# A 128-row K tile loaded by transfers of 64, 32, 16 and 8 rows, once in each of two layers

## The chip, the core and the metric

The kernel runs on one core of a Trainium2 chip. The core has engines that run beside each other, each with its own instruction stream: TensorE (PE, with its weight loads PEld), VectorE (DVE), ScalarE (ACT), GpSimd (POOL) and SyncE (SP), which issues the data transfers. Sixteen DMA engines carry them. The on-chip memory has 128 rows (partitions). The metric is the time of one execution on the device in microseconds (us); lower is better.

## The reference

Two layers, each an attention block over a cache and a small mixer block, for one new token in each of two batch entries:

```python
def _A_ref(x, k_cache, v_cache, wq, wo):
    B, Sq, D = x.shape            # 2, 1, 576
    H, Dh = 32, 128
    q = (x @ wq).reshape(B, Sq, H, Dh).transpose(0, 2, 1, 3)
    scores = jnp.einsum("bhqd,bhkd->bhqk", q, k_cache) * (Dh ** -0.5)
    p = _softmax(scores, axis=-1)
    o = jnp.einsum("bhqk,bhkd->bhqd", p, v_cache)
    return o.transpose(0, 2, 1, 3).reshape(B, Sq, H * Dh) @ wo
...
x = A_x
x = x + _A_ref(_layernorm(x, axis=-1), A_k_cache, A_v_cache, A_wq, A_wo)
x = x + _B_ref(_layernorm(x, axis=-1), B_w1, B_w2, B_w3, B_w4)
x = x + _A_ref(_layernorm(x, axis=-1), A_k_cache, A_v_cache, A_wq, A_wo)
x = x + _B_ref(_layernorm(x, axis=-1), B_w1, B_w2, B_w3, B_w4)
return x
```

The caches are [2, 32, 16384, 128] in bf16. Each of the 2 x 32 = 64 units (one head of one batch entry) has a K of 4 MB and a V of 4 MB, and both layers read all of them: 2 x 64 x 8 MB, apart from five tiles that the second layer still finds on the chip whole or in part. `_B_ref` adds small products with w1 to w4 (576 and 4608 wide).

## The kernel before

**Tiles.** The K or the V of a unit is one tile: 128 rows of 32 KB, where row p holds 128 neighbouring positions of 128 values. `mem` has six slots for such tiles (`NSLOT`, L334, L376). `plan_all` writes down all transfers of the kernel in the order in which they are to be issued, each with its place in `mem`: `plan_tile` (L426) and `plan_piece` (L435) for the caches, others for the weights. A tile in one piece is one entry with one transfer of 128 rows and the semaphore of its slot (`tile0` to `tile5`). The order is K of a unit, then V of the unit before (`tile_order`, L569). Layer 0 takes the units from 0 to 63, layer 1 takes 62, 63, 61 and then 0 to 60 (`order`, L565).

**Issue.** `Store.pump` (L286) hands out the entries in order, as soon as the slot of the first one is free; `Store.release` (L322) frees a slot when the last instruction that reads it is placed, and pumps again. `Graph.dma` (L88) makes of an entry one SyncE operation that starts each transfer of its list, and each adds 16 to the semaphore when it has landed (L101); the value that readers wait for is counted by the number of transfers:

```python
self.dma_count[sem] += 16 * len(starts)
o.val = self.dma_count[sem]
h = self.dma_sems[sem]

def fn(sp):
    for dst, src in starts:
        sp.dma_start(dst, src).then_inc(h, 16)
```

All transfers stand on SyncE's one queue, in the order of the plan.

**Landing.** `landed` (L1194) places a relay on GpSimd: it waits for the tile's semaphore and tells TensorE, and for K tiles VectorE too. In the profile a wait for the relay is named POOLq L202.

**Attention of one unit.** Half of a K tile's columns are transposed on TensorE (L1241), copied out by ScalarE (L1253) and multiplied with the query (L1267); VectorE does the other half with an elementwise product (L1287) and a sum (L1291). Then come the maximum over all rows on GpSimd (L1307), the exponentials on ScalarE (L1319, L1322), and the product with V on TensorE (L1361). Most units run inside loops on the three compute engines; SyncE and GpSimd are written out in full. A unit's V is used one unit later than its K.

**Between the layers and at the end** the weights wo, w3, w4, wq (and w1 at the end) pass through the same slots in smaller pieces, and the products with them (L874, L751, L768) follow each other.

The first small weight, w2, is loaded at the start by two transfers: four blocks of 128 rows of 1152 B, and a tail of 64 rows of 1152 B, which go to rows 64 to 127.

Of the kernel before, what the change touches and what calls it, by code (L numbers as in the profile page):

```python
# [328 lines left out]
class KB:  # L329
# [11 lines left out]
    PARKED = 5  # L341
    GONE = 72
    RAW = 2
    TURNS = {("w3", 0): 1, ("w3", 1): 1, ("w3", 2): 1, ("w4", 1): 1, ("w4", 3): 1, ("w4", 6): 1, ("w4", 8): 1,
             ("wq", 0): 1, ("wq", 1): 1, ("wq", 2): 1}

# [25 lines left out]
    def _alloc(self):  # L372
# [44 lines left out]
        self.quad = misc[:, 20:24]  # L417
        self.raw = misc[:, 24:24 + self.RAW * (1 + 3 * B) // 2].bitcast(BF16).rearrange("p (k c) -> p k c", k=self.RAW)
        self.cor = [self.prod[:, 1280 + 2 * MT * B * i:1280 + 2 * MT * B * (i + 1)].bitcast(FP32) for i in range(2)]
# [3 lines left out]
        self.mps = ps("mps", [128, 512], FP32)  # L423


    def plan_tile(self, t, u, slot, cuts=(), skip=0):  # L426

        b, hh = u % self.B, u // self.B
        src = (self.K if t == "k" else self.V)[b, hh].rearrange("(p j) d -> p (j d)", p=128)
        cuts = [0, *cuts, self.NB]  # L430
        for a, z in zip(cuts[:-1], cuts[1:]):
            if a >= skip:
                self.plan_piece(t, u, slot * self.TILE, src, a, z - a)

    def plan_piece(self, t, u, base, src, a, n):  # L435
        sem = f"tile{base // self.TILE}" if n == self.NB else f"piece{base // self.TILE}_{a}_{n}"
        self.store.plan((t, u, a, n), sem, base + 256 * a, 256 * n,
                        [(lambda m: m, src[:, a * 128:(a + n) * 128])])

    def plan_cols(self, nm, l, w, parts):  # L440

# [57 lines left out]
    def plan_all(self):  # L499

        T, U, n = self.TILE, self.U, self.KT - 1
        row, w3r, wqr = 2 * self.D, 2 * self.F, 2 * 128 * self.H
        H, MT = self.H, self.MT
        self.parts = {}
        self.plan_cols("wq", 0, self.wq, self.whole(self.wq, [4 * T + wqr * k for k in range(self.KT)]))
        self.plan_small("w2", 0, self.w2, 4 * T + wqr * n + wqr // 2, (0, 64))

        tiles = self.tile_order(0)
        place = [i % 6 for i in range(len(tiles))]
        place[-1] = 2  # L510
        half, quarter = self.BP, self.BP // 2
        for (t, u), slot in zip(tiles, place):
            self.plan_tile(t, u, slot, (half, half + quarter) if (t, u) == ("v", U - 1) else ())
        last = {tile: slot for tile, slot in zip(tiles, place)}
        third = U - self.CARRY - 1
        assert last["k", third] == 1 and last["v", third] == 4

        self.cuts = {}
        P = 4 * row
        a, c = [4 * T + P * i for i in range(4)], [T, T + P]  # L520
        assert 256 * self.GONE == 4 * P and 256 * 8 * self.PARKED >= 2 * P and 256 * 8 * self.NKT >= P
        turn = iter([*a, c[0]] + [a[0], a[1], c[1], a[2], a[3], c[0]] * 6)
        h = MT // 2
        self.cuts["wo", 0] = [(i, i + 4, next(turn)) for i in range(0, 32, 4)]
        halves = lambda n: [(k, m, z, next(turn)) for k in range(self.KT - 1) for m, z in ((0, n), (n, 2 * n))] + \
                           [(self.KT - 1, 0, 2 * n, next(turn))]
        w3 = halves(h)
        self.groups = [(0, 4, 8, 12, 16, 18), (0, 8, 12, 16, 18)]
        g = self.groups[0]
        self.cuts["w4", 0] = [(h * i + p, h * i + q, next(turn)) for i in range(2) for p, q in zip(g[:-1], g[1:])]  # L530
        self.plan_rows("wo", 0, self.wo, self.cuts["wo", 0])
        self.plan_cols("w3", 0, self.w3, w3)
        self.plan_groups("w4", 0, self.w4, self.cuts["w4", 0])
        self.plan_cols("wq", 1, self.wq, halves(H // 2))

        b, hh = third % self.B, third // self.B
        tiles = self.tile_order(1)
        b2, h2 = tiles[0][1] % self.B, tiles[0][1] // self.B
        for i in (1, 2, 3, None, 0):
            if i is None:  # L540
                self.plan_piece(*tiles[0], T, self.K[b2, h2].rearrange("(p j) d -> p (j d)", p=128), 0, quarter)
            else:
                self.plan_piece("v", third, 4 * T, self.V[b, hh].rearrange("(p j) d -> p (j d)", p=128),
                                i * self.GONE // 4, self.GONE // 4)
        place = [(3, 4, 5, 0, 2, 1)[i % 6] for i in range(len(tiles))]
        for i, (t, u) in enumerate(tiles):
            if (t, u) != ("v", third):
                self.plan_tile(t, u, place[i], (quarter, half, half + quarter) if i == 0 else
                               (half,) if i == len(tiles) - 1 else (), 0 if i else quarter)
        self.cuts["wo", 1] = [(0, 11, 2 * T), (11, 22, 2 * T + 11 * row), (22, 32, 0)]  # L550
        at = 10 * row
        w4_at = T + 2 * w3r + w3r // 2
        self.cuts["w4", 1] = [(0, 8, w4_at)] + \
                             [(a, b, 3 * T + (a - 8) * row) for a, b in ((8, 16), (16, 26), (26, 30), (30, 34), (34, 36))]
        self.plan_rows("wo", 1, self.wo, self.cuts["wo", 1])
        self.plan_cols("w3", 1, self.w3, self.whole(self.w3, [at, at + w3r, T, T + w3r, T + 2 * w3r]))
        self.plan_groups("w4", 1, self.w4, self.cuts["w4", 1])
        w1_at = 2 * T
        for i, k in enumerate((0, 2)):
            self.store.plan(("w1", 1, i), f"w1_{i}", w1_at + k * row, 2 * row, [  # L560
                (lambda m: m.rearrange("p (k n) -> p k n", n=self.D),
                 self.w1[k * 128:(k + 2) * 128, :].rearrange("(k p) n -> p k n", p=128))])
        self.store.plan(("w1", 1, 2), "w1_2", w1_at + 4 * row, row, [(lambda m: m[self.TL:, :], self.w1[4 * 128:, :])])
# [168 lines left out]
    def unscaled(self):  # L732

        R, B = self.RAW, self.B
        hi, lo = self.raw[:, :, 1:1 + B], self.raw[:, :, 1 + B:1 + 2 * B]
# [4 lines left out]
    def cols_chunk(self, w, l, k, out, pk, n, rhs, rk, cols, first, last=False, held=False):  # L740
# [15 lines left out]
        if l == (1 if w == "wq" else 0):  # L756
            self.turn(self.TURNS.get((w, k), 0), settle=not held)

# [60 lines left out]
    def hs_projection(self):  # L819
# [16 lines left out]
        self.copy_psum(self.hs, "hs")  # L836
        B, R = self.B, self.RAW
        self.dv(lambda e: e.tensor_copy(out=self.raw[:, :, 1 + 2 * B:], in_=self.hs[:, 0:R, :]),
# [22 lines left out]
    def rows_projection(self, w, l, rhs, rk):  # L861
# [4 lines left out]
        for i, (a, b, _) in enumerate(cuts):  # L866
# [14 lines left out]
            if l == 0:  # L881
                if (w, i) == ("wo", 1):
                    self.park(self.order(0)[self.U - self.CARRY - 1], self.NKT, self.PARKED)
                self.turn(self.TURNS.get((w, i), 0))

    def z_projection(self, l):
        B, KT, MT, R = self.B, self.KT, self.MT, self.RAW
        MB, w = MT * B, 1 + 3 * B
# [568 lines left out]
```

## Time and profile before

| | |
|---|---|
| time, median of 3 runs | 2550.05 us (2549.99 to 2550.48) |
| profiled execution, its time | 2549.84 us |
| profiled execution, its span | 2548.1 us, first to last instruction |
| DVE busy | 1897.0 us, 74% |
| PE / PEld busy | 1614.7 us, 63% / 1580.7 us, 62% |
| ACT busy | 1204.2 us, 47% |
| read from HBM | 1092.37 MB, 429 GB/s over the span |
| K tiles in one transfer | 124, median 40.7 us from issue to landing |
| V tiles in one transfer | 123, median 49.6 us from issue to landing |

How to read it: the span is cut into 40 equal slices of 63.7 us, and each digit is a busy share in tenths. "DMA" is the mean busy share of the 16 DMA engines, "GB/s" what they moved. "xN" counts instructions, packets or issues. "A <- B" reads "A waited for B". In the view of stretches ("755.84:1183.33 ...") the columns are the stretch, its length, the busy time and count of PE, PEld, DVE, ACT and POOL, the granted TensorE clock, the DMA share and GB/s. In the DMA view a packet is one row of a transfer, "under 512 B" are the marks at the end of each engine's part, and each queue's line has packets, MB and the share of 16 engines over the stretch. In the view of waits the numbers are us in total, times, and the longest in us.

### The profile page before, as it was taken

The page shows a single profiled execution, that of the slowest core. Times are in us where ns is not written, and L with a number is a line of the kernel's source. Part 1 is how long each engine was busy: PE and PEld are TensorE (multiplying, and loading weights), DVE is VectorE, ACT ScalarE, POOL GpSimd, SP SyncE. Part 2 cuts the span into 40 slices and gives each one's busy share as a digit, 9 for nine tenths or more (in the row PEclk, how much of TensorE's full clock was granted, in tenths as well). Part 3 has the DMA queues.
Part 4 walks back from the last instruction along what each step waited for, and adds up shares of the span by engine and source line. Part 5 has one row for each costly group of instructions (what it writes and reads, how often), then busy time and mean ns, then how long its engine had stood idle before and what let it go on. Part 6 is the DMA issues. An engine that isn't in the chain of part 4 may idle for free.

```text
span 2548.1 us, 74893 instructions
## 1 busy us (share of the span) xinstructions
PE 1614.7 (63%) x34407; PEld 1580.7 (62%) x34407; DVE 1897.0 (74%) x2062; ACT 1204.2 (47%) x1810; POOL 53.5 (2%) x151
## 2 busy tenths in 40 slices
PE   4666666656666666666777766656665666666566
PEld 3666666656666665666667666656665665666566
DVE  5877777777777777777648877777777777777774
ACT  3544544444454444445435544444454444445442
POOL 0000000000000000000000000000000000000000
PEclk8555555555555555555656555565555555555555
DMA  9999999999999999999999999999999999999999
GB/s 410 428 433 431 432 432 431 433 431 433 430 432 432 432 432 431 433 431 432 419 411 427 432 431 432 432 432 432 432 432 432 432 432 432 432 433 431 433 431 386
DMA packets 46928, 1093.19 MB, mean 429 GB/s; under 512 B 5140, under 2 KB 6296, under 8 KB 12440
## 3 DMA queue, kind: packets, MB, share of 16 engines
q1 hardware_dynamic: 46872, 1092.40, 100.0%
q8 instruction: 41, 0.67, 0.1%
q14 instruction: 15, 0.12, 0.0%
HBM read 1092.37 MB, written 0.00 MB: 429 GB/s over the span
## 4 chain that ended last, share of the span: by engine, by line
DMA 66%; DVE 23%; PE 5%; issue 5%; SPq 1%; ACT 0%; DVEq 0%; POOLq 0%
DMA mem<-in_A_k_cache_dram 63%; DVE s_dve L1291 12%; DVE prod L1287 9%; PE tps L1241 2%; PE mps L1361 2%; DMA mem<-in_B_w_dram 1%; DMA mem<-in_A_wo_dram 1%; PE sps L1267 1%; SPq L101 1%; PE sps L1212 1%; DVE diag L1208 0%; DVE l L1339 0%; DVE q_col L1205 0%; DMA mem<-in_A_wq_dram 0%; DVE mx L1302 0%
## 5 line engine op out<-in xcount | busy, mean ns | idle before, releaser
L1253 ACT ACTIVATE kt<-tps 128x1024 bf16<-128x1024 bf16 x992 | 1002.9, 1023 | 878.0 <-PE tps L1241 859.5
L1291 DVE TENSOR_REDUCE s_dve<-prod 128x16 f32<-128x2048 bf16 x504 | 1152.1, 2286 | 17.3
L1241 PE MATMUL tps<-ident,mem 128*128 128x128 bf16 x8192 | 1000.0, 300 | 141.3 <-POOLq L202 135.2
L1287 DVE TENSOR_TENSOR prod<-mem,qb 128x2048 bf16<-128x2048 bf16 x504 | 616.8, 1224 | 525.4 <-POOLq L202 493.9
L1361 PE MATMUL mps<-p,mem 128*128 128x1 bf16 x16384 | 512.2, 166 | 549.7 <-POOLq L202 519.3
L1241 PEld LDWEIGHTS tps<-ident,mem 128*128 128x128 bf16 x8192 | 761.3, 136 | 151.1 <-POOLq L202 145.0
L1361 PEld LDWEIGHTS mps<-p,mem 128*128 128x128 bf16 x16384 | 487.5, 104 | 558.3 <-ACT p L1322 552.2
L1267 PEld LDWEIGHTS sps<-q_col,kt 128*128 128x128 bf16 x7936 | 399.5, 113 | 0.8 <-ACT kt L1253 0.4
L1267 PE MATMUL sps<-q_col,kt 128*128 128x1 bf16 x7936 | 388.1, 170 | 0.4 <-issue 0.3
L1212 PE MATMUL sps<-diag,ones_bf 128*128 128x128 bf16 x127 | 36.5, 287 | 195.4 <-DVE diag L1208 195.4
L1212 PEld LDWEIGHTS sps<-diag,ones_bf 128*128 128x128 bf16 x127 | 13.2, 104 | 205.6 <-DVE diag L1208 205.6
L1316 ACT ACTIVATE mx<-mx 128x1 f32<-128x1 f32 x128 | 26.0, 203 | 236.2 <-POOL mx L1307 236.2
L1307 POOL PARTITION_ALL_REDUCE mx<-mx x128 | 51.1, 400 | 2441.9 <-DVE mx L1305 2323.7
L1215 ACT ACTIVATE qb<-sps 128x128 bf16<-128x128 f32 x127 | 35.2, 277 | 137.3 <-PE sps L1212 137.3
L1319 ACT ACTIVATE p<-s_dve,mx 128x64 bf16<-128x64 f32 x126 | 43.8, 348 | 4.1
L1253 ACT ACTIVATE mem<-tps 128x1024 bf16<-128x1024 bf16 x32 | 32.0, 1025 | 22.0 <-PE tps L1241 19.6
L1322 ACT ACTIVATE p<-sps,mx 128x64 bf16<-128x64 f32 x128 | 37.7, 294 | 0.1
L1302 DVE TENSOR_REDUCE mx<-sps 128x1 f32<-128x64 f32 x128 | 27.6, 216 | 7.5 <-PE sps L1267 7.5
L874 PE MATMUL mps<-prod,mem 128*128 128x2 bf16 x680 | 22.1, 166 | 14.5 <-DMA mem<-in_B_w_dram 8.8
L1208 DVE TENSOR_SCALAR diag<-ident,q_f 128x128 bf16<-128x128 bf16 x127 | 31.1, 245 | 0.0
L874 PEld LDWEIGHTS mps<-prod,mem 128*128 128x128 bf16 x680 | 20.6, 105 | 16.2 <-DMA mem<-in_B_w_dram 7.5
L707 ACT ACTIVATE misc<-misc 128x2 f32<-128x2 f32 x8 | 2.4, 296 | 51.4 <-DVE misc L705 51.4
(117 smaller groups left out, 293.4 us busy)
## 6 DMA issues: line engine op xcount, KB each, us to landing
mem<-in_A_k_cache_dram SPq DMA_DIRECT2D x124, 4096.0 KB, 40.7
mem<-in_A_v_cache_dram SPq DMA_DIRECT2D x123, 4096.0 KB, 49.6
mem<-in_B_w_dram SPq DMA_DIRECT2D x21, 576.0 KB, 7.7
mem<-in_B_w_dram SPq DMA_DIRECT2D x7, 1152.0 KB, 33.9
mem<-in_A_v_cache_dram SPq DMA_DIRECT2D x3, 2048.0 KB, 40.4
mem<-in_A_wq_dram SPq DMA_DIRECT2D x10, 512.0 KB, 6.5
mem<-in_A_wo_dram SPq DMA_DIRECT2D x8, 576.0 KB, 19.3
mem<-in_A_wq_dram SPq DMA_DIRECT2D x4, 1024.0 KB, 8.0
```

The lines of the kernel that those rows point to most:

```text
L874: ins = pe.matmul(self.mps[:, t * B:(t + 1) * B], lhsT=buf[:, o:o + 128], rhs=rhs(k), start=(k == 0 and t == 0), stop=(k == last), skip_gr ...
L1212: self.pe(lambda pe: pe.matmul(qps, lhsT=self.ones_bf[:, :], rhs=self.diag[:, :], start=True, stop=True, skip_group_check=True), reads=["o ...
L1215: self.act(lambda e: e.activation(out=self.qb[i][:, :], in_=qps, func=ACT.Copy), reads=[("qps", i)], writes=[("qb", i)], sig=("qb", i))
L1241: ins = pe.transpose(self.tps[t][:, j * 128:(j + 1) * 128], buf[:, j * 128:(j + 1) * 128], self.ident[:, :])
L1253: self.act(lambda e: e.activation(out=out, in_=self.tps[t][:, :], func=ACT.Copy), reads=[("tps", t)], writes=keys, sig=("evac", c, t, k))
L1267: ins = pe.matmul(self.sps[sp][:, c * self.CH + j:c * self.CH + j + 1], lhsT=buf[:, j * 128:(j + 1) * 128], rhs=self.q_col[:, sp:sp + 1], ...
L1287: self.dv(lambda e: e.tensor_tensor(out=prod, in0=buf.rearrange("p (j d) -> p j d", d=128), in1=qbc, op=ALU.mult), reads=[("qb", r)] + key ...
L1291: self.dv(lambda e: e.tensor_reduce(out=sd[:, c0:c0 + DB], in_=prod, axis=AX.X, op=ALU.add), reads=["prod"], writes=[("s_dve", r)], sig=(" ...
L1307: self.pool(lambda e: e.partition_all_reduce(mx[3], mx[2], channels=128, reduce_op=ROP.max), reads=[("mx2", i)], writes=[("mx3", i)])
L1319: self.act(lambda e: e.activation(out=p[:, n:self.NB], in_=self.s_dve[i][:, 0:self.NB - n], func=ACT.Exp, bias=mx[4], scale=self.scale, ac ...
L1322: self.act(lambda e: e.activation(out=p[:, 0:n], in_=self.sps[i][:, 0:n], func=ACT.Exp, bias=mx[4], scale=self.scale, accum_out=self.ls[:, ...
L1361: ins = pe.matmul(self.mps[:, 448:449], lhsT=buf[:, j * 128:(j + 1) * 128], rhs=p[:, col:col + 1], start=b == 0, stop=b == self.NB - 1, sk ...
```

## The change

`plan_tile` is told the layer, and looks up in a table `SHARE` whether a tile is to be split by rows. `runs` gives the splits: 128 rows for nearly all tiles as before; for a share of 2 transfers of 64, 32 and four times 8 rows; for a share of 1 transfers of 64, 32, 16 and twice 8 rows. They stand in one entry of the plan, so one after the other on SyncE's queue, on the semaphore of the tile's slot. Two tiles have a share: K of unit 40 in layer 0 (2) and K of unit 20 in layer 1 (1). In a 128-row transfer every DMA engine moves eight rows; with the splits half of them move ten (nine) and half six (seven). The place of every row in `mem` stays, and so does all compute.

```diff
+    SHARE = {(0, "k", 40): 2, (1, "k", 20): 1}
...
-    def plan_tile(self, t, u, slot, cuts=(), skip=0):
+    def plan_tile(self, l, t, u, slot, cuts=(), skip=0):
...
-                self.plan_piece(t, u, slot * self.TILE, src, a, z - a)
+                self.plan_piece(t, u, slot * self.TILE, src, a, z - a, self.SHARE.get((l, t, u), 0))
...
+    @staticmethod
+    def runs(share):
+
+        sizes, left = [], 16 * (8 - share)
+        for n in (128, 64, 32, 16):
+            if left >= n:
+                sizes.append(n)
+                left -= n
+        sizes += [8] * (2 * share)
+        return [(sum(sizes[:i]), sum(sizes[:i + 1])) for i in range(len(sizes))]
+
+    def plan_piece(self, t, u, base, src, a, n, share=0):
...
-                        [(lambda m: m, src[:, a * 128:(a + n) * 128])])
+                        [(lambda m, lo=lo, hi=hi: m[lo:hi, :], src[lo:hi, a * 128:(a + n) * 128])
+                         for lo, hi in self.runs(share)])
...
-            self.plan_tile(t, u, slot, (half, half + quarter) if (t, u) == ("v", U - 1) else ())
+            self.plan_tile(0, t, u, slot, (half, half + quarter) if (t, u) == ("v", U - 1) else ())
...
-                self.plan_tile(t, u, place[i], (quarter, half, half + quarter) if i == 0 else
+                self.plan_tile(1, t, u, place[i], (quarter, half, half + quarter) if i == 0 else
```

In SyncE's stream the K tile of unit 40 stands between the V tiles of units 38 and 39; the order of everything else is as before, and no other engine's instructions change.

More of the change, by code (lines that the diff above doesn't have):

```diff
@@ L432, in plan_tile @@
             if a >= skip:
-                self.plan_piece(t, u, slot * self.TILE, src, a, z - a)
-    def plan_piece(self, t, u, base, src, a, n):
+                self.plan_piece(t, u, slot * self.TILE, src, a, z - a, self.SHARE.get((l, t, u), 0))
[9 more added lines that the diff above has]
+    def plan_piece(self, t, u, base, src, a, n, share=0):
         sem = f"tile{base // self.TILE}" if n == self.NB else f"piece{base // self.TILE}_{a}_{n}"
         self.store.plan((t, u, a, n), sem, base + 256 * a, 256 * n,
-                        [(lambda m: m, src[:, a * 128:(a + n) * 128])])
+                        [(lambda m, lo=lo, hi=hi: m[lo:hi, :], src[lo:hi, a * 128:(a + n) * 128])
+                         for lo, hi in self.runs(share)])
     def plan_cols(self, nm, l, w, parts):
```

## The prediction

> **What bounds the kernel now.** I read the summary of the page first (busy shares, slices, queues, the chain that ended last), then the windows around the two edited tiles, then the waits.
>
> ```profile
> span 2548.1 us, 74893 instructions
> ...
> DMA  9999999999999999999999999999999999999999
> GB/s 410 428 433 431 432 432 431 433 431 433 430 432 432 432 432 431 433 431 432 419 411 427 432 431 432 432 432 432 432 432 432 432 432 432 432 433 431 433 431 386
> ...
> q1 hardware_dynamic: 46872, 1092.40, 100.0%
> q8 instruction: 41, 0.67, 0.1%
> ...
> DMA 66%; DVE 23%; PE 5%; issue 5%; SPq 1%; ACT 0%; DVEq 0%; POOLq 0%
> ```
> ```profile
> 755.84:1183.33 427.49, 269.44 (x5660) 264.53 (x5658) 326.12 (x330) 204.88 (x309) 7.87 (x22) 0.57 1.00 432
> 1183.33:1311.40 128.07, 91.50 (x2000) 87.44 (x1997) 72.79 (x140) 61.79 (x88) 3.83 (x5) 0.58 1.01 416
> 1687.00:2486.00 799.00, 502.80 (x10592) 493.66 (x10593) 607.75 (x618) 382.00 (x576) 14.42 (x41) 0.57 1.00 432
> ```
> ```profile
> DVE prod L1287 <- POOLq L202: 493.9, 114, 4.4
> ...
> POOL mx L1307 <- DVE mx L1305: 419.6, 22, 19.1
> ...
> PE mps L1361 <- POOLq L202: 99.7, 22, 5.1
> ...
> DVE prod L1287 <- POOLq L202: 96.1, 22, 4.4
> ```
>
> The DMA engines set the time. In both long streams their share is 1.00 at 432 GB/s, while the busiest compute engine, DVE, works 326.12 of 427.49 us (fifth number of the window's row). DVE's pause stands once per unit (a head of a batch entry), up to 4.4 us, and ends with GpSimd's relay (POOLq L202), which tells that a K tile has landed. So no unit has its data early: compute takes each tile as it lands. The span is 2548.1 us in a run of 2549.84 us, 1.74 us around it; that run lies 0.21 us under the median of 2550.05.
>
> ```profile
> 755.84 0.33 SPq L101 DMA_DIRECT2D mem<-in_A_k_cache_dram  x1
> 756.69 0.33 SPq L101 DMA_DIRECT2D mem<-in_A_v_cache_dram  x1
> 775.29 0.33 SPq L101 DMA_DIRECT2D mem<-in_A_k_cache_dram  x1
> ...
> 1670.09 0.33 SPq L101 DMA_DIRECT2D mem<-in_A_k_cache_dram  x1
> 1670.95 0.33 SPq L101 DMA_DIRECT2D mem<-in_A_v_cache_dram  x1
> ```
> ```profile
> DMA packets 1330, 38.83 MB, mean 431 GB/s; under 512 B 145, under 2 KB 145, under 8 KB 145
> ...
> q1 hardware_dynamic: 1330, 38.83, 100.2%
> ...
> mem<-in_A_k_cache_dram SPq DMA_DIRECT2D x5, 4096.0 KB, 40.7
> mem<-in_A_v_cache_dram SPq DMA_DIRECT2D x5, 4096.0 KB, 49.6
> ```
>
> The first fence is SyncE's timeline where the edited tiles are issued: layer 0's K tile of unit 40 at 755.84 us, layer 1's of unit 20 at 1670.09 (counted along its issues). One K and one V tile go out every 19.45 us, so a tile takes the DMA engines 9.72. The second is the DMA view of 2150 to 2240 us: 1330 - 145 = 1185 packets of 32 KB (one row of a tile each) share 100.2% of 16 engines x 90 us, which is 1.22 us a row and engine; eight rows to an engine make the 9.72. A K tile lands 40.7 us after its issue, so about four tiles stand queued: an engine that falls behind never lacks work, and never gets its delay back.
>
> **The change part by part.** *Issues.* Layer 0's tile goes out as six transfers for one, layer 1's as five.
>
> ```profile
> 2486.02 1.28 SPq L101 DMA_DIRECT2D mem<-in_A_wo_dram  x3
> ```
> ```profile
> SPq L101 <- PE sps L1267: 2142.2, 124, 18.6
> ```
>
> Three issues in a row take 1.28 us, 0.43 each, so five more are 2.1 us and four more 1.7. They stand ahead of the V tile of the same step, which then is issued 2.1 us later of its 49.6; SyncE itself waits 17.3 us per K tile (2142.2 / 124) for a slot. Cost 0 under that queue; 3.8 us with it gone. The wait on the tile is on one semaphore, now of 96 (80) counts, asked by the same relay; behind it on GpSimd stand the relay of the V tile and the maximum over partitions (L1307) of the unit before, and PE, DVE and ACT wait for those. They shift with the landing, none adds to it.
>
> *Rows.* Bytes stay the same. A 128-row transfer gives each engine 8 rows. By the change's description the 8-row transfers all go to one half of the engines, which then move 4 + 2 + 4 = 10 rows (layer 1: 4 + 2 + 1 + 2 = 9), the others 6 (7). As the engines never idle in the stream, the late half keeps its delay to the end of its layer, where all data must be in: 2 x 1.215 = +2.4 us, and +1.2 in layer 1.
>
> *Transfers of fewer rows.* The page has one kind to compare: the 72 KB tail of the first small weight, 64 rows of 1152 B, just ahead of the first K tile.
>
> ```profile
> mem<-in_B_w_dram SPq DMA_DIRECT2D x2, 72.0 KB, 13.3
> ```
> ```profile
> DMA packets 85, 0.10 MB, mean 387 GB/s; under 512 B 1, under 2 KB 85, under 8 KB 85
> ...
> q1 hardware_dynamic: 85, 0.10, 107.3%
> ```
> ```profile
> DMA packets 191, 0.79 MB, mean 464 GB/s; under 512 B 28, under 2 KB 172, under 8 KB 172
> ...
> q1 hardware_dynamic: 191, 0.79, 131.1%
> ```
> ```profile
> DMA packets 30, 0.98 MB, mean 410 GB/s; under 512 B 0, under 2 KB 0, under 8 KB 0
> ...
> q1 hardware_dynamic: 30, 0.98, 95.5%
> ```
> ```profile
> DMA packets 123, 1.29 MB, mean 514 GB/s; under 512 B 17, under 2 KB 17, under 8 KB 17
> ...
> q1 hardware_dynamic: 123, 1.29, 121.5%
> ```
>
> These are DMA views of 14.9 to 15.15, 15.3 to 17.0, 17.0 to 19.4 and 1326 to 1328.5 us (a packet counts whole where it starts, so shares pass 100%). In the first, 84 packets of 1152 B take 107.3% x 16 x 0.25 = 4.3 us: 0.051 each. In the second the tail is loaded and the first 191 - 172 = 19 rows of 32 KB begin: 35.7 us, less 144 x 0.051, leaves 28.3, or 1.49 a row with the 28 end marks in it. In the third a row takes 36.7 / 30 = 1.22 again. So about 19 x 0.27 = 5.1 us over 16 engines, 0.32 each, went to the tail, whose own four rows per engine take 0.20: it occupied the engines 2.6 times as long as its bytes should. Small packets ahead of large ones alone don't do that: in the fourth, 128-row transfers of 8 KB rows pass into 32 KB rows, and 1.29 MB at 26.9 GB/s (38.83 MB / 1443 us) would take 48.0 us and takes 48.6. I read it thus: what the engines write into shares a path by groups of rows; in a 128-row transfer each engine has a path of its own, while 64 rows reach half of the paths, two engines to each.
>
> With that, a transfer that reaches n of the 16 paths lasts 16/n times its bytes' time. The 64 rows of 32 KB: between 4.86 us (no sharing) and 12.6 (2.6 times); I take twice, 9.72, since part of the 0.32 may be the start of the K stream. For 32, 16 and 8 rows nothing in the trace is nearer. At the low end they take 2.43, 1.215 and 1.215 us per engine; at the high end their rows lie on the paths of 4, 2 and 1 engines of a 128-row transfer, and each lasts 9.72 again. I take half of the high end, 4.86: neighbouring rows need not lie on one path (64 of them came out at two engines to a path), and the middle of 1.2 and 9.7 is 5.5. Every one of these steps stands on the path of the late half. Layer 0: 9.72 + 5 x 4.86 = 34.0 for 9.72, +24.3 us (low +2.4, high 12.6 + 5 x 9.72 - 9.72 = +51.5). Layer 1: 9.72 + 4 x 4.86 = 29.2, +19.4 us (low +1.2, high 12.6 + 4 x 9.72 - 9.72 = +41.8).
>
> [...]
>
> *Where the delay goes.* The edited tile lands up to 24 us late; compute, which waits for every tile, shifts by that, SyncE's next issues with it. The six-row half has 40.7 us of queue, so it lives on; the ten-row half works on without a pause. Layer 0's end waits for it, with no slack: the turn from 1183 to 1311 us still moves 416 GB/s. There the halves meet again (the early one waits), so layer 1 adds its own delay. Sum: 2549.84 + 24.3 + 19.4 = 2593.5 us.
>
> **Rivals.**
>
> *A. The engines are independent, and the change evens them out: no slower.* For it: 16 engines at 1.22 us a row hold 432 GB/s in every slice, as if each were limited by itself; the instruction queue's 41 packets (0.67 MB) fall on some engines and not on others, and if all fell in the half that now gets fewer rows, that half was late by 0.67 MB / 8 / 26.9 GB/s = 3.1 us. Against: the 1.49 us rows. Price: +2.4 + 1.2 if the ten-row half was the late one, at best -3.1: 2546.7 to 2553.5, in the middle about 2549. It decides if the rows of the split tile still take 1.22 us.
>
> *B. Only the 64-row transfers pay; the small ones find free paths,* since engines that arrive at different times need not collide. Layer 0: 4.86 + 2.4, layer 1: 4.86 + 1.2: 2563.2. Against: all 16 engines are within a few us of each other.
>
> *C. Rows next to each other share one path each time,* the high ends: 2549.84 + 51.5 + 41.8 = 2643.1. For it: 2.6 is above 2. Against: for 64 rows no more than two engines need share a path, and nothing in the trace shows eight on one.
>
> *D. The change doesn't do what it says:* the four 8-row transfers fall on fewer engines than eight, say four with two rows each time: 4 x 1.215 more in layer 0, 2 x 1.215 in layer 1 even without shared paths, 3.6 + 7.3: 2560.7. No run here shows an 8-row transfer. [...]
>
> **How the numbers follow.** Main case 0.62 (2575 to 2606: 4.86 for a small transfer may be 3 to 6, nine of them, and the engines' spread softens collisions), A 0.17, B 0.10, C 0.08, D 0.03. Time 2593.5. The range 2548 to 2606 takes in the main case's, B, D and the upper part of A, and leaves out C and the gains. A change under 0.2% (5.1 us) can't be told from none here. Faster by that needs more than A's best gain: 0.02. Within: A nearly whole, 0.16. Slower: 0.82.
>
> **What would show it.** Right: in the DMA view from about 784 to 830 us (layer 0) the 32 KB rows average well over 1.22 us, and GB/s falls as half the engines wait; K issues after the edited tile stand some 24 us later than before, counted from the start, and stay so to the turn; a second shift of some 19 us comes from 1700 us on; DVE's longest wait on POOLq L202 grows from 4.4 to some 25 us. The V tile's issue right behind shows whether SyncE's extra 2.1 us are hidden. Wrong: rows at 1.22 us there and shifts within 3 us (A); a shift near 7 (B), near 51 (C); or a delay that shrinks before the turn, which would mean that engines can catch up.

## The result, and the profile after

| | before | after |
|---|---|---|
| time, median of 6 runs each | 2550.16 us (2549.99 to 2551.15) | 2594.63 us (2592.13 to 2596.54) |
| ratio to before, 95% interval | | 1.0174 (1.0163 to 1.0185) |
| profiled execution, its time / its span | 2549.84 / 2548.1 us | 2593.43 / 2591.7 us |
| DVE / ACT busy | 1897.0 / 1204.2 us | 1897.3 / 1204.6 us |

The change costs 44.5 us, or 1.74%. The forecast was 2593.5 us. Line numbers of the changed kernel stand 13 above those of before in the compute functions.

The first fence is the summary of the page of the changed kernel.

```profile
span 2591.7 us, 74902 instructions
...
DMA  9999999999999999999999999999999999999999
GB/s 412 427 432 431 431 432 432 431 433 432 431 432 276 432 431 432 432 431 432 404 409 427 432 431 431 433 331 416 432 432 431 432 432 432 431 432 432 431 432 385
...
q1 hardware_dynamic: 46968, 1092.40, 99.9%
...
DMA 63%; DVE 22%; issue 5%; PE 5%; another core or an unknown queue 4%; SPq 1%; ACT 0%; DVEq 0%; POOL 0%; POOLq 0%
```

Bytes and the compute engines' work are what they were, and the DMA engines show as busy as before in every slice. But the bytes that they move drop in two places: slice 13 (from 778 us on) has 276 GB/s, slices 27 and 28 (from 1685 us) 331 and 416. A slice is 64.8 us long, so the first lacks (432 - 276) / 432 x 64.8 = 23.4 us' worth of bytes, the other two (101 + 16) / 432 x 64.8 = 17.6. So here an engine counts as busy while its rows take longer (2.73 and 3.83 us for 1.22, below): the busy share doesn't tell it, GB/s does.

Where the time goes in is read from SyncE's timeline, whose issues can be paired one by one. The columns are the start in us, the duration, and the issue. First the kernel before, then the changed one.

```profile
775.29 0.33 SPq L101 DMA_DIRECT2D mem<-in_A_k_cache_dram  x1
...
794.70 0.33 SPq L101 DMA_DIRECT2D mem<-in_A_k_cache_dram  x1
...
814.12 0.33 SPq L101 DMA_DIRECT2D mem<-in_A_k_cache_dram  x1
...
1236.05 4.59 SPq L101 DMA_DIRECT2D mem<-in_A_wo_dram  x4
...
1708.95 0.33 SPq L101 DMA_DIRECT2D mem<-in_A_k_cache_dram  x1
...
1728.36 0.33 SPq L101 DMA_DIRECT2D mem<-in_A_k_cache_dram  x1
...
2546.50 0.28 SPq L101 DMA_DIRECT2D out_dram<-prod  x1
```
```profile
755.77 2.47 SPq L101 DMA_DIRECT2D mem<-in_A_k_cache_dram  x6
758.29 0.35 SPq L101 DMA_DIRECT2D mem<-in_A_v_cache_dram  x1
775.22 0.35 SPq L101 DMA_DIRECT2D mem<-in_A_k_cache_dram  x1
...
797.67 0.33 SPq L101 DMA_DIRECT2D mem<-in_A_k_cache_dram  x1
...
841.26 0.33 SPq L101 DMA_DIRECT2D mem<-in_A_k_cache_dram  x1
...
1262.85 4.60 SPq L101 DMA_DIRECT2D mem<-in_A_wo_dram  x4
...
1695.89 2.28 SPq L101 DMA_DIRECT2D mem<-in_A_k_cache_dram  x5
...
1736.49 0.33 SPq L101 DMA_DIRECT2D mem<-in_A_k_cache_dram  x1
...
1772.31 0.33 SPq L101 DMA_DIRECT2D mem<-in_A_k_cache_dram  x1
...
2589.80 0.28 SPq L101 DMA_DIRECT2D out_dram<-prod  x1
```

The six issues take 2.47 us instead of 0.33, and the next K tile still goes out on time (775.22 for 775.29): the queue hides them. Then the issue of 794.70 is 3.0 us late and that of 814.12 is 27.1 late: a slot comes free when compute is through with its tile, and compute waits for the split tile. At the end of layer 0 the issue of wo is 26.8 us late, so next to nothing of it is caught up in the 422 us from the issue at 841.26. The split tile of layer 1 is issued 25.8 us late (1695.89 for 1670.09), so the turn between the layers gave back 1.0. Two K issues later the delay is 27.5, and then 43.9 (1772.31 for 1728.36); the output goes out 43.3 us late. So the two tiles cost 27 and 18 us.

The DMA view of the changed kernel from 784 to 794 and from 800 to 820 us shows the rows themselves (a packet is a row; those under 512 B are end marks):

```profile
DMA packets 72, 1.90 MB, mean 190 GB/s; under 512 B 14, under 2 KB 14, under 8 KB 14
...
q1 hardware_dynamic: 72, 1.90, 98.9%
...
DMA packets 122, 2.62 MB, mean 131 GB/s; under 512 B 42, under 2 KB 42, under 8 KB 42
...
q1 hardware_dynamic: 122, 2.62, 95.8%
```

72 - 14 = 58 rows of 32 KB take 98.9% of 16 x 10 us, 2.73 us each; later 80 rows take 95.8% of 16 x 20, 3.83 us each. Before it was 1.22. The waits of the changed kernel from 755 to 1000 us (total, times, longest):

```profile
DVE prod L1300 <- POOLq L202: 79.3, 12, 31.6
```

VectorE's longest wait for the landing of a K tile went from 4.4 to 31.6 us.

### The profile page after: what moved, and what is told of

Read it like the earlier page. It is cut to its first block, busy times and chain, and to the rows that moved or that the text cites. A ratio compares the mean times of both kernels' runs of the same rounds, so it can differ in the third digit from the quotient of the medians.

```text
span 2591.7 us, 74902 instructions
## 1 busy us (share of the span) xinstructions
PE 1614.4 (62%) x34407; PEld 1580.7 (61%) x34407; DVE 1897.3 (73%) x2062; ACT 1204.6 (46%) x1810; POOL 53.7 (2%) x151
## 4 chain that ended last, share of the span: by engine, by line
DMA 63%; DVE 22%; issue 5%; PE 5%; another core or an unknown queue 4%; SPq 1%; ACT 0%; DVEq 0%; POOL 0%; POOLq 0%
DMA mem<-in_A_k_cache_dram 61%; DVE s_dve L1304 12%; DVE prod L1300 8%; PE tps L1254 2%; PE mps L1374 2%; DMA mem<-in_B_w_dram 1%; SPq L101 1%; PE sps L1280 1%; PE sps L1225 0%; DVE diag L1221 0%; DVE mx L1315 0%; DMA mem<-in_A_wq_dram 0%; DVE l L1352 0%; DMA mem<-in_A_wo_dram 0%
## 5 line engine op out<-in xcount | busy, mean ns | idle before, releaser
L1304 DVE TENSOR_REDUCE s_dve<-prod 128x16 f32<-128x2048 bf16 x504 | 1152.1, 2286 | 17.3
L1225 PEld LDWEIGHTS sps<-diag,ones_bf 128*128 128x128 bf16 x127 | 13.2, 104 | 201.5 <-DVE diag L1221 201.5
L1315 DVE TENSOR_REDUCE mx<-sps 128x1 f32<-128x64 f32 x128 | 27.7, 216 | 8.2 <-PE sps L1280 8.2
L887 PE MATMUL mps<-prod,mem 128*128 128x2 bf16 x680 | 22.0, 166 | 13.2 <-DMA mem<-in_B_w_dram 8.0
L887 PEld LDWEIGHTS mps<-prod,mem 128*128 128x128 bf16 x680 | 20.5, 104 | 14.8 <-DMA mem<-in_B_w_dram 6.8
```

Source lines behind the costliest of these rows:

```text
L887: ins = pe.matmul(self.mps[:, t * B:(t + 1) * B], lhsT=buf[:, o:o + 128], rhs=rhs(k), start=(k == 0 and t == 0), stop=(k == last), skip_gr ...
L1225: self.pe(lambda pe: pe.matmul(qps, lhsT=self.ones_bf[:, :], rhs=self.diag[:, :], start=True, stop=True, skip_group_check=True), reads=["o ...
L1304: self.dv(lambda e: e.tensor_reduce(out=sd[:, c0:c0 + DB], in_=prod, axis=AX.X, op=ALU.add), reads=["prod"], writes=[("s_dve", r)], sig=(" ...
```

## The experiments

The question left by the two traces is why the rows last so long: because of the on-chip rows that a transfer covers, the place in HBM, the number of transfers, their size, or the ten rows on half of the engines. A path is, as in the prediction, what several on-chip rows are supposed to share; no view shows one, only row times and delays. All experiments change K of unit 40 in layer 0 alone, except the second of the last pair. The first column of numbers is the delay of the K issue that stands at 814.12 us before, read as above; then the output's issue, and the time against runs of the kernel before beside them.

| experiment | K issue late, us | output late, us | time, median | ratio (95% interval) |
|---|---|---|---|---|
| change in layer 0 alone | 25.0 | 25.1 | 2575.82 (before 2550.07) | 1.0102 (1.0085 to 1.0119) |
| six transfers by columns | 0.4 | 0.1 | 2550.28 (2550.07) | 1.0001 (0.9991 to 1.0011) |
| 64 + 64 rows | 13.4 | 14.2 | 2564.27 (2550.07) | 1.0056 (1.0040 to 1.0073) |
| 8 rows as every fourth of 96 to 127 | 21.0 | 20.8 | 2571.26 (2550.07) | 1.0084 (1.0067 to 1.0101) |
| four times 32 rows | 13.6 | 13.6 | 2564.75 (2550.55) | 1.0057 (1.0040 to 1.0074) |
| 8 rows as every fourth of 0 to 31 | 14.8 | 15.9 | 2565.70 (2550.55) | 1.0057 (1.0040 to 1.0073) |
| every fourth row on chip only | 22.6 | 23.6 | 2571.88 (2550.55) | 1.0083 (1.0066 to 1.0100) |
| every fourth row in HBM only | 26.7 | 27.7 | 2576.14 (2550.55) | 1.0098 (1.0081 to 1.0115) |
| 64 from the middle + 32 + 32 | 8.9 | 8.1 | 2559.54 (2549.89) | 1.0039 (1.0025 to 1.0053) |
| 64 + 32 + 32 in order | 15.6 | 14.3 | 2565.49 (2549.89) | 1.0062 (1.0045 to 1.0079) |
| load moved with all paths in use, layer 0 | 6.6 | 6.7 | 2557.87 (2550.06) | 1.0033 (1.0020 to 1.0045) |
| the same in both layers | 7.5 | 14.7 | 2564.14 (2550.06) | 1.0052 (1.0039 to 1.0066) |

The split of the change was made three times in layer 0 with the same on-chip rows (27.1, 25.0 and, with other HBM rows, 26.7): single delays scatter by 1 us or so either way, and smaller differences are not read. The expectations take the delay from the issues further on towards the turn, where it stands 0.2 to 0.3 us lower than in the table (13.2 for 13.4, 24.7 for 25.0).

**The change in layer 0 alone.**

```diff
-    SHARE = {(0, "k", 40): 2, (1, "k", 20): 1}
+    SHARE = {(0, "k", 40): 2}
```

> The change in layer 0 alone (K of unit 40 in transfers of 64, 32 and four times 8 rows; layer 1 as before). In the changed kernel the issues were 26.9 us late from this tile to the end of layer 0, 25.8 us after the turn between the layers, and 43.7 us at the end. Paths shared by neighbouring rows (my theory): the two tiles cost their own prices, one after the other, so here the issues are 26.9 us late before the turn, 25.8 after it and at the end, and the time is 25.8 us over that of the kernel before, about 2576. Rival, the two delays hang together (the second tile only pays because the halves of the engines are already apart from the first): the end is late by 26.9 or by 43.7 us less what layer 1's tile costs alone, so that a shift at the end other than 25.8 would speak for it.

SyncE's timeline of this kernel:

```profile
839.16 0.33 SPq L101 DMA_DIRECT2D mem<-in_A_k_cache_dram  x1
...
2571.63 0.29 SPq L101 DMA_DIRECT2D out_dram<-prod  x1
```

25.0 us late at once and 25.1 at the end: this tile pays for itself, and layer 1's adds its 18 us on top. The 1 us that the turn gave back in the changed kernel doesn't show here.

How many engines a transfer of 8 rows takes can be counted. The DMA packets of the whole run, before and with this change:

```profile
DMA packets 46928, 1093.19 MB, mean 429 GB/s; under 512 B 5140, under 2 KB 6296, under 8 KB 12440
...
DMA packets 46976, 1093.19 MB, mean 425 GB/s; under 512 B 5188, under 2 KB 6344, under 8 KB 12488
```

There are 48 more end marks. A transfer of 128 rows leaves 16 (the next experiment has five more of them and 5220 marks, 80 more), and so do one of 64 rows and one of 32 (5156 marks with two of 64, 5188 with four of 32). So the four of 8 rows leave 48 + 16 - 2 x 16 = 32, eight each. As 16 engines leave 16 marks, I read one mark per engine: a transfer of 8 rows runs on eight engines, one row each.

**Six transfers by columns,** the control for their number and size.

```diff
+        at = [0, 64, 96, 104, 112, 120, 128]
+        return [(slice(0, 128), c, z) for c, z in zip(at[:-1], at[1:])]
```

> K of unit 40 in layer 0 goes out as six transfers again, with bytes in the same proportion of 64, 32 and four times 8, but each has all 128 rows and a share of the columns (rows of 16, 8 and four times 2 KB). Paths theory: a transfer of 128 rows gives each engine its own path, so nothing is shared: +0 us (within 1), time as before, about 2550. Rival, each further transfer costs about 5 us of the queue whatever its rows (26.9 us for five more: 5.4 each): +26.9 us, about 2576. Rival, small packets are slow: the quarter of the tile that lies in packets of 2 KB would be slower, which a delay between 1 and 10 us would show.

SyncE's timeline:

```profile
755.81 4.59 SPq L101 DMA_DIRECT2D mem<-in_A_k_cache_dram  x6
760.45 8.46 SPq L101 DMA_DIRECT2D mem<-in_A_v_cache_dram  x1
775.27 6.11 SPq L101 DMA_DIRECT2D mem<-in_A_k_cache_dram  x1
781.42 5.43 SPq L101 DMA_DIRECT2D mem<-in_A_v_cache_dram  x1
...
814.48 0.33 SPq L101 DMA_DIRECT2D mem<-in_A_k_cache_dram  x1
...
2546.55 0.29 SPq L101 DMA_DIRECT2D out_dram<-prod  x1
```

Nothing: six transfers with the same bytes each cost 0.1 us at the output as long as each has all 128 rows. Their issue took 4.59 us, and the three issues behind them 8.46, 6.11 and 5.43 us for 0.33 each (why, is not shown): 23.3 us more of SyncE's time than before, at a place where it otherwise waits for slots (17.3 us per K tile). So neither the number of transfers, nor their completion, nor the six issues are the price.

**Two transfers of 64 rows.**

```diff
+        return [slice(0, 64), slice(64, 128)]
```

> K of unit 40 in layer 0 as two transfers of 64 rows each. Every engine moves four rows of each, eight in all, so the engines are loaded evenly. Paths theory: 64 neighbouring rows reach half of the paths, so each of the two lasts 9.72 us where its bytes would take 4.86: +9.7 us before the turn, about 2559 in all. Rival, only the uneven load of the halves of the engines matters (ten rows and six): +0. Rival, a price per transfer: one more transfer, +5.4 us. Rival, twice the price of the small weight's tail (2.6 for 2): 2 x 12.6 - 9.7 = +15.5 us.

SyncE's timeline, then the DMA view from 786 to 806 us:

```profile
827.49 0.33 SPq L101 DMA_DIRECT2D mem<-in_A_k_cache_dram  x1
```
```profile
DMA packets 160, 4.19 MB, mean 210 GB/s; under 512 B 32, under 2 KB 32, under 8 KB 32
...
q1 hardware_dynamic: 160, 4.19, 99.7%
```

Two transfers with 16 end marks each (32) have all 16 engines at work, on eight rows each if the rows are spread evenly, so the uneven load is not needed for a loss. 160 - 32 = 128 rows, as many as a tile has, take 99.7% of 320 us: 2.49 each, 2.05 times 1.215. Eight of them make +10.2 us per engine, near the +9.7 of the theory; the measured 13.4 is 3.2 more, and nearer to the +15.5 of the last rival. Where it lies shows in the queue's lines from 780 to 840 us, before and here:

```profile
q1 hardware_dynamic: 887, 25.92, 100.4%
...
q1 hardware_dynamic: 715, 20.28, 100.4%
```

The engines are as busy, and move 5.64 MB less, which is 13.1 us of the stream at 432 GB/s. So nearly all of the delay is rows that last longer, and 3 us of it lie in rows before and after those 128: from 780 to 786 us, where the tile before ends, the four slices of 1.5 us have 437, 415, 328 and 262 GB/s. I read it so that engines a few us apart write 128-row and 64-row transfers at the same time (in the kernel before, the 16 end marks of one tile spread over three steps of 2 us, from 752 to 758 us: 1, 10 and 5). So the two together take 9.72 + 13.4 = 23.1 us, 11.6 each: between the 9.72 that I took and the high end of 12.6.

**Four transfers of 32 rows.**

```diff
+        return [slice(i, i + 32) for i in range(0, 128, 32)]
```

> K of unit 40 in layer 0 as four transfers of 32 rows: two rows to an engine each time, eight in all. Two transfers of 64 rows measured 13.2 us more. Paths theory in the form that 32 neighbouring rows reach as many paths as 64 (half of them): the four together cost as the two of 64, +13 us before the turn, and the rows last some 2.5 us each. Paths theory in the form of half the high end (4.86 us for each transfer of 32 rows): 4 x 4.86 - 9.72 = +9.7, or with the excess that two64 showed likewise +13. Rival, neighbouring rows fill one path after the other (32 rows reach four paths): 4 x 9.72 - 9.72 = +29 us, and rows of some 4.9 us. Rival, a price per transfer: +3 x 13.2 = +40 us.

The DMA view from 784 to 790 us:

```profile
DMA packets 55, 1.21 MB, mean 202 GB/s; under 512 B 18, under 2 KB 18, under 8 KB 18
...
q1 hardware_dynamic: 55, 1.21, 100.1%
```

13.6 us late, as two of 64, and 37 rows at 96.1 / 37 = 2.60 us, where the filling of one path after the other asked for 4.9. So a row in transfers of 32 neighbouring rows lasts about as long as in those of 64 (2.49 us), which I read as half of the paths, not a quarter; one such transfer takes (9.72 + 13.6) / 4 = 5.8 us. The two rivals, 29 and 40 us, fall. (The two forms of the theory ask for the same here: 4.86 is twice the 2.43 of 32 rows.)

**Other rows for the four 8-row transfers.** Sizes, number and order as in the change.

```diff
+        return [slice(0, 64), slice(64, 96)] + [slice(96 + i, 128, 4) for i in range(4)]
```

> K of unit 40 in layer 0 as 64, 32 and four times 8 rows, as in the change, but the four small transfers take every fourth row (96, 100, ... 124; 97, 101, ...; and so on) instead of eight neighbouring rows each. Number, order, size and engines of the transfers are as in the change. Paths theory: eight rows that stand four apart, over 32 rows, lie on more paths than eight neighbouring ones, and collide less: from 26.9 us the delay falls to about 15 us (9.7 us stay with the 64 and the 32 rows, and some 5 us for the small ones, which still find only the paths of 32 rows), about 2564 in all. Rival, the price comes from the number or size of the transfers, or from the ten rows of half of the engines: unchanged, +26.9 us before the turn and about 2576 in all.

```diff
+        return [slice(64, 128), slice(32, 64)] + [slice(i, 32, 4) for i in range(4)]
```

> K of unit 40 in layer 0 as 64 rows (64 to 127), 32 rows (32 to 63) and four times 8 rows, every fourth of rows 0 to 31. Number, sizes and engines as in the experiment with every fourth of rows 96 to 127, which was 20.7 us late; only which rows differs. If the 8-row transfers go to the engines that write rows 0 to 63 in a 128-row transfer, then they write here only the paths which these engines have for themselves, and meet no one: what is left is the price of the 64 and the 32 rows and two rows more on these engines, about +13 us, with no rows over 2.7 us once the 32 rows are through. Rival, those 8-row transfers cost by their number or size, or any eight of them within 32 rows cost the same: +20.7 us. Rival, the 8-row transfers go to the engines of rows 64 to 127: then the experiment before had no meeting in them and this one has: more than 20.7.

The DMA views from 800 to 806 us, in which the 8-row transfers begin (rows of the next tile are among those counted): the change in layer 0 alone, every fourth row of 96 to 127, and every fourth row of 0 to 31.

```profile
DMA packets 41, 0.82 MB, mean 137 GB/s; under 512 B 16, under 2 KB 16, under 8 KB 16
...
q1 hardware_dynamic: 41, 0.82, 103.9%
```
```profile
DMA packets 40, 0.85 MB, mean 142 GB/s; under 512 B 14, under 2 KB 14, under 8 KB 14
...
q1 hardware_dynamic: 40, 0.85, 93.7%
```
```profile
DMA packets 64, 1.28 MB, mean 213 GB/s; under 512 B 25, under 2 KB 25, under 8 KB 25
...
q1 hardware_dynamic: 64, 1.28, 96.8%
```

In 16 x 6 = 96 us of engine time: 25 rows at 99.7 / 25 = 3.99 us, 26 rows at 3.46, 39 rows at 2.38. Transfers of the same number and size go with shorter rows when their on-chip rows lie further apart, and with shorter ones again on the other half of the on-chip rows. The delays follow: 25.0, 21.0, 14.8 (for the last some 13 were expected). In the last the 8-row transfers are as good as free: 64 rows and 32 rows alone take 11.6 + 5.8 = 17.4 us, and 9.72 + 14.8 - 17.4 = 7.1 is left for four transfers whose bytes need 4.86. For every fourth row of 96 to 127 I had expected about 15 us in all: the direction was right, the size 6 us short. That these engines write rows 0 to 63 in a 128-row transfer is how I read the 14.8: no view shows which rows an engine writes. The rival that they serve rows 64 to 127 asked for more than 20.7.

**On chip or in HBM.** One side of the four small transfers takes every fourth row, the other neighbouring rows. In each pair of slices the first is the on-chip side, the second the HBM side.

```diff
+        return [(slice(0, 64),) * 2, (slice(64, 96),) * 2] + [(slice(96 + i, 128, 4), slice(96 + 8 * i, 104 + 8 * i)) for i in range(4)]
```
```diff
+        return [(slice(0, 64),) * 2, (slice(64, 96),) * 2] + [(slice(96 + 8 * i, 104 + 8 * i), slice(96 + i, 128, 4)) for i in range(4)]
```

> The change in layer 0 alone with the four 8-row transfers reading eight neighbouring rows of HBM each, as in the change, but writing to every fourth on-chip row (96, 100, ... 124 and so on). So rows 96 to 127 of K of unit 40 in layer 0 lie in another order than the reference has them; the rest is computed as before. If the paths belong to the on-chip rows (theory): as with every fourth row on both sides, +20.7 us before the turn, rows of at most 3.7 us in the view of 800 to 820 us. If they belong to HBM (neighbouring rows lie in one bank or on one channel): as in the change, +24.7 us in layer 0 alone, and rows of 3.4 to 4.1 us.

> The mirror of the run before: the four 8-row transfers read every fourth row of HBM and write eight neighbouring on-chip rows each, with rows 96 to 127 of K of unit 40 in layer 0 in another order than the reference has them. If the paths belong to the on-chip rows: +24.7 us as with the change in layer 0 alone. If they belong to HBM: +20.7 us.

The DMA views from 800 to 806 us, every fourth row on chip first, then every fourth row in HBM:

```profile
DMA packets 43, 0.92 MB, mean 153 GB/s; under 512 B 15, under 2 KB 15, under 8 KB 15
...
q1 hardware_dynamic: 43, 0.92, 102.3%
```
```profile
DMA packets 37, 0.75 MB, mean 126 GB/s; under 512 B 14, under 2 KB 14, under 8 KB 14
...
q1 hardware_dynamic: 37, 0.75, 100.3%
```

28 rows at 3.51 us with the on-chip rows apart, 23 at 4.19 with the HBM rows apart. The delays are 22.6 and 26.7; with both sides apart and both together it was 21.0 and 25.0. Each pair differs by 4.1, the times agree (2575.82 - 2571.26 = 4.6 and 2576.14 - 2571.88 = 4.3), and the on-chip side alone decides: rows apart in HBM go with 1.6 us less in one pair (21.0 for 22.6) and 1.7 more in the other (26.7 for 25.0), which is scatter.

**64 rows from the middle.** The last test of which rows share a path, with its control.

```diff
+        return [slice(32, 96), slice(0, 32), slice(96, 128)]
```
```diff
+        return [slice(0, 64), slice(64, 96), slice(96, 128)]
```

> K of unit 40 in layer 0 as 64 rows from the middle (32 to 95), then 32 rows (0 to 31) and 32 rows (96 to 127). Two transfers of 64 rows, 0 to 63 and 64 to 127, were 13.2 us late, four of 32 rows 13.4. [...] Rival, a transfer of 64 rows reaches half of the paths wherever it lies (its engines share by their number, not by the rows): +13.3 us. Rival, the cut out of line with the halves costs more: over 13.3.

> The control for the run before: the same sizes in the same order, 64, 32 and 32 rows, but rows 0 to 63, 64 to 95, 96 to 127. All theories: half of two transfers of 64 rows (13.2) and half of four of 32 rows (13.4), +13.3 us.

The DMA views from 784 to 788 us, in which the 64-row transfer runs, first with rows 32 to 95, then with rows 0 to 63:

```profile
DMA packets 65, 1.70 MB, mean 426 GB/s; under 512 B 13, under 2 KB 13, under 8 KB 13
...
q1 hardware_dynamic: 65, 1.70, 101.6%
```
```profile
DMA packets 36, 0.88 MB, mean 221 GB/s; under 512 B 9, under 2 KB 9, under 8 KB 9
...
q1 hardware_dynamic: 36, 0.88, 117.5%
```

52 rows at 65.0 / 52 = 1.25 us and 426 GB/s against 27 rows at 75.2 / 27 = 2.79 and 221: a 64-row transfer of rows 32 to 95 runs at full rate, one of rows 0 to 63 at half of it. The rival that 64 rows run at half the rate wherever they lie (+13.3 us) falls. My estimate for the first kernel was this: if rows 32 to 95 cost their bytes alone, only the two transfers of 32 rows pay, half of the 13.4 us of four (read towards the turn), which is 6.7. The delays differ by 15.6 - 8.9 = 6.7 us (6.2 at the output), as the two estimates do (13.3 - 6.7); both lie 2.2 to 2.3 above them (1.4 and 1.0 at the output), which stays unexplained. Which single rows share a path is not shown by these runs; they show that rows 32 to 95, from both halves of the tile, run at full rate together, and rows 0 to 63 don't.

**Can load be moved between engines at no loss?** The tile goes out as one transfer of 128 rows with 96 of the 128 column blocks, and sixteen of 8 rows with the last 32 blocks, so that, with all sixteen on the same eight engines, half of the engines move 320 KB and half 192 KB as in the change.

```diff
+        return [(slice(0, 128), 0, 96)] + [(slice(g + i, g + 32, 4), 96, 128) for g in (0, 32, 64, 96) for i in range(4)]
```

> Layer 0 alone, the same load of the engines as with the change (half of them move 320 KB of the K tile of unit 40, half 192 KB), but every path stays in use: 128 rows with 96 of the 128 column blocks, and then sixteen transfers of 8 rows (every fourth row of 32) with the last 32 blocks, 64 KB each. If evening out the load of the engines is worth something where collisions are kept small (rival, and the only way in which such a split could pay): earlier by 1 to 2.4 us, 2547.7 to 2549. If the late half is the one that gets more: +2.4 us. Paths theory: the transfers for rows 0 to 63 write paths that their engines have for themselves (no price), those for rows 64 to 127 meet the other eight engines, which have gone on to the next tile: 8 x 64 KB per 8 engines at half the rate, which is 2.4 us more, so +2 to +5 us, about 2554. A price for each transfer (16 more; the control by columns measured 0.0 us for five) would give more than 10 us.

> As the run before, with K of unit 20 in layer 1 split in the same way too. Paths theory: the price twice, +4 to +10 us, about 2558. Evening out pays: 2545 to 2548. The late half gets more: +4.8 us.

6.6 us late in one layer, 14.7 at the output in both: a loss in both, larger than the 2 to 5 that I had for one. The queue's line from 780 to 840 us, in one layer:

```profile
q1 hardware_dynamic: 1084, 24.09, 100.1%
```

That is 1.83 MB less than the 25.92 of before, or 4.2 us of the stream. Half of the engines then move 64 KB more each, two rows' worth or 2.4 us; if this is the late half, the sum is the 6.6 measured. Read so, the collisions cost 4.2, more than the 2.4 that I had worked out for them, and the load moved is paid for on top. The same sum gives 12.3 + 2.4 = 14.7 us for every fourth row of 0 to 31 (14.8 measured; 20.61 MB) and 21.0 + 2.4 = 23.4 for the change in layer 0 alone (25.0 measured; 16.84 MB). Moving load is not worth anything here even where collisions are few.

## Why the prediction was right, step by step

*The issues cost nothing:* right. V behind the split tile went out 1.6 us later (758.29 for 756.69), the next K on time; with 23.3 us more of issue in the control by columns the output moved by 0.1.

*A 64-row transfer lasts twice its bytes' time:* right in kind for rows 0 to 63 and 64 to 127 (32 to 95 ran at full rate, 1.25 us a row), low in size. Its rows last 2.05 times as long, and with the rows of the neighbouring tiles it takes 11.6 us, where I took 9.72 and had 12.6 as the high end. By the whole delay (11.6 / 4.86 = 2.4 times) the 72 KB tail's 2.6 was nearer than my 2; by the rows alone (2.05) the 2 was.

*32, 16 and 8 rows take 4.86 each, half of the high end:* the choice was a middle between bounds far apart, and in the mean it came out. One of 32 rows takes 5.8. The three splits with neighbouring 8-row transfers are 26.3 us late in the mean, so the four take 9.72 + 26.3 - 11.6 - 5.8 = 18.6 us, 4.7 each. In layer 1 the one of 16 and the two of 8 rows take 9.72 + 18.1 - 11.6 - 5.8 = 10.4, 3.5 each, less than my 4.86; the one of 16 was not measured by itself. But 4.86 is no property of the size: other rows of the same count take 1.8 each (7.1 / 4). With on-chip rows four apart, four transfers of the same size cost 4.1 us less; I read it so that eight neighbouring rows lie on few paths, while eight engines (by the end marks) write them.

*Layer sums:* layer 0 +24.3 forecast, +27.1 measured in the changed kernel and 25.0 alone; layer 1 +19.4 forecast, 43.9 - 25.8 = +18.1 measured. The errors have opposite signs, so that the total of 43.7 fits better than its parts: 43.3 at the output. That it came this near is luck: each of the two 64-row transfers was set 1.9 us too low, the small ones of layer 1 together 3.2 us too high (16.2 for 19.4), and the 1 us of the turn was not in the sum.

*The delay is kept to the end of the layer, and the second adds to it:* right. It stays at 26.8 to 27.1 us up to the turn; of 27 us the turn gave back 1.

*VectorE's longest wait grows to some 25 us:* wrong in the sum, not in the place. The 4.4 us of before stay and the delay comes on top: 4.4 + 27.1 = 31.5, measured 31.6.

*The rivals.* A (independent engines, evened out) falls with the row times of 2.5 to 4 us; its best gain was looked for by moving load with all paths in use, and was a loss (7.8 us by the median time). What was said for it is not quite so: 432 GB/s stood in the long streams, not in every slice (386 to 433), and no view shows on which engines the 41 packets of the instruction queue fell. B (only the 64-row transfers pay) falls with the four of 32 rows and with the 3.99 us rows. C (each small transfer on one path) asked for 51 us in layer 0; rows of 4 us and the four of 32 rows exclude it. D (fewer than eight engines) falls with the end marks: eight for each transfer of 8 rows. It falls by the row times too: with 8-row transfers as cheap as 1.8 us, two rows on each of four engines would take 2.4 at least.

## What to carry to other kernels

In a stream that is bound by transfers, the number of transfers and their issues cost nothing here, under some 40 us of queue (0.1 us at the output for six transfers by columns); the on-chip rows that each one covers decide. Cut a tile by columns and keep 128 rows in each transfer; if it must be cut by rows, measure which rows go well together (32 to 95 ran at 1.25 us a row and 426 GB/s, 0 to 63 at 2.79 and 221), and count a delay in full: of 27.1 us here 26.8 were left at the end of the layer. A DMA share near 100% doesn't show that bytes flow (it was 98.9% here at 190 GB/s): look at GB/s and at the time of one row.

## What was not expected of the hardware

- Transfers of rows 0 to 63 and 64 to 127, read here as two engines on one path, lose a little more than half of the rate: 2.49 us a row for 1.215 (2.05 times), over 128 rows.
- A split tile costs more than its own rows: of the 13.4 us for 64 + 64 rows, 128 rows at 2.49 us make 10.2, and the other 3.2 lie in the rows around them.
- Eight neighbouring on-chip rows and eight rows four apart, in transfers of the same number and size, differ by 4.1 us over four transfers, twice (26.7 for 22.6 us, 25.0 for 21.0 us); with every fourth of rows 0 to 31 it was another 6.2 us less (14.8).
